# Moving work between engines and banks in a linear-attention and feed-forward kernel: last q on two engines, one load moved, single banks for two products

## The chip, the core and the metric

The kernel runs on one core of a Trainium2 chip. A core has TensorE (matrix products), VectorE, ScalarE and GpSimd (element by element), SyncE (issues transfers), 16 DMA engines, and a PSUM of 8 banks of 512 float32 columns into which TensorE writes. The metric is the device time of one execution in microseconds; the profile is of one such execution. In the profile's lines PE is TensorE, PEld its weight loads, DVE VectorE, ACT ScalarE, POOL GpSimd, SP SyncE; L594 is line 594 of the kernel before.

## What is computed

Linear attention with cosine weights, then a gated feed-forward block. Cut to what matters:

```python
# q, k, v: (8 batches, 8 heads, 576 positions, 64), float32
theta = pi / 2 * arange(576) / 576
phi(x) = concat([relu(x) * cos(theta), relu(x) * sin(theta)])       # 64 -> 128 features
kv  = einsum('bhsf,bhsd->bhfd', phi(k), v);  z = phi(k).sum(positions)
att = (phi(q) @ kv) / (phi(q) @ z + 1e-6)
x   = att.transpose(0, 2, 1, 3).reshape(4608, 512)
g   = x @ w_gate                                                     # 512 -> 1536
out = (g * sigmoid(g) * (x @ w_val)) @ w_out                         # -> (4608, 512)
```

## The kernel before

The 4608 tokens are 36 tiles of 128, four tiles to a **group**, groups 0 to 8. While TensorE does the feed-forward block of one group, the attention of later tiles is worked in between. The kernel hands out its work by **slots**: a group has 16, 12 for the gate and value products and 4 for the output products, and `at(slot, ...)` puts a piece of work behind the products of that slot, in program order on every engine. Batch b has `s0 = 16 * (b - 1)` and `p0 = s0 - 16`; a row of a table says in which slots its parts stand:

```python
# batch: (slots of q's weighting, slot of q's turning, slots of k's and v's preparation, all from p0; k-v product, from s0)
ROW = {2: ([16, 16, 17, 17], 18, (20, 21, 21, 22), 8), 3: ([12, 13, 14, 15], 18, (20, 20, 21, 21), 6), ...
       7: ([4, 4, 5, 5, 6, 6, ..., 12, 12], 15, (12, 13, 14, 15), 3)}
TILES = {2: (1, 9, 10, 11), 3: (5, 9, 10, 11), ...}      # slots of a group's four attention tiles
GATE = (5, 6, 7, 8)                                       # groups whose gate products go by quarters
AHEAD = 5
```

q is rectified and weighted with cos and sin into `r_q` (one buffer for all batches), and turned by a DMA transpose into `phit`. For batches 2 to 6 ScalarE rectifies and VectorE weights (`phi_q`, 4 of each); for batch 7 ScalarE does both in 18 parts:

```python
def phi_q_part(b, c, w):                                                                 # L296
    nc.scalar.activation(out=st[b, "q"][:, :, c, w], in_=raws[b, "q"][:, :, c], func=AF.Relu,
                         scale=csk[:, c, w:w + 1])                                       # L299
def qturn_dma(b, e):
    nc.sync.dma_start_transpose(out=phit[b][:, e]..., in_=st[b, "q"][e * 64:(e + 1) * 64]...)   # L322
```

The k-v product of a batch takes two neighbouring banks, half `e` in each; ScalarE and VectorE then copy it out, each from both banks:

```python
def kv_mm(b):
    ps = st[b, "kvps"] = take(2, ("kv", b))
    for j, c in ...:
        for i in range(2):
            for e in range(2):
                nc.tensor.matmul(out=ps[i * 64:(i + 1) * 64, e, ...], lhsT=raws[b, "k"]..., rhs=v2s...)  # L349
def kv_out2(b):
    def part(w, eng):
        for i in range(2):
            eng(out=kv2s[b % 2][w * 64:(w + 1) * 64, :, :, i], in_=ps[i * 64:(i + 1) * 64, :, :, w])     # L373
    part(0, nc.scalar.copy)
    if b - 1 in GATE:
        behind.append(lambda: (part(1, nc.vector.tensor_copy), kv_free(b)))
    else:
        part(1, nc.vector.tensor_copy)
```

An attention tile is 8 or 16 small products into two banks (`a_tile2`, L472), whose result VectorE divides into `x` (`x_of`: L486, L495, L499); a DMA transpose turns it into `xT` (`x_turn`, L578), which the feed-forward products of the next group read.

The feed-forward block of groups 1 to 4 (L594 products, L600 silu, L605 product with the value) and by quarters from group 5 on, with fewer products and more sums (`while behind` works off what was put into a list):

```python
def ffn_by_quarters(tg, slot_of):
    for u in range(3):
        product(a, ...); nc.scalar.copy(out=b, in_=a)             # products L652, copy L681
        product(e, ...); nc.scalar.copy(out=m7, in_=e)            # L685
        V(...); done()                                            # value products L665; done() works off a slot
        product(b, ...); nc.vector.tensor_tensor(out=c, in0=m7, in1=b, op=ALU.add)        # L691
        while behind: behind.pop(0)()
        product(a, ...); silu(u, 1, 0, a); V(...); done()         # silu: ScalarE, L658
        product(b, ...); nc.vector.tensor_tensor(out=m7, ...)     # L700
        while behind: behind.pop(0)()
        ...
        mul(u, 0, 0); mul(u, 1, 0)                                # VectorE, ht <- sg * value, L670
        ...
```

The output products (L767, from group 2 on by quarters, L826) end with the results in `ob` and eight stores to memory, from GpSimd's queue (L749). That queue also issues the loads of q, k and v of later batches:

```python
def load_behind(b):                       # in slot p0 + 3 (b < 5) or p0 + 1
    nc.gpsimd.tensor_copy(out=hold2, in_=phit[b - 1]...)          # L1038: waits for the turned q of the batch before
    if b < AHEAD: load(b, "q")
    if b > 3: load_kv(b)
    if AHEAD <= b + 1 < B: load(b + 1, "q")
```

Of the kernel before, what the change touches and what calls it, by code (L numbers as in the profile page):

```python
# [14 lines left out]
ALU = mybir.AluOpType  # L15
# [3 lines left out]
def kernel(  # L19
# [10 lines left out]
    nc = tc.nc  # L30
# [20 lines left out]
    KH = KC // 2  # L51
    GATE = (5, 6, 7, 8)
    AHEAD = 5
    WSUM = (32, 39, 49, 64)
    ROW = {2: ([16, 16, 17, 17], 18, (20, 21, 21, 22), 8), 3: ([12, 13, 14, 15], 18, (20, 20, 21, 21), 6), 4: ([12, 12, 12, 14], 15, (15, 16, 17, 18), 5), 5: ([12, 12, 12, 14], 15, (15, 16, 17, 17), 5), 6: ([6, 8, 11, 12], 14, (13, 14, 14, 17), 3), 7: ([4, 4, 5, 5, 6, 6, 7, 7, 8, 8, 9, 9, 10, 10, 11, 11, 12, 12], 15, (12, 13, 14, 15), 3)}
    TILES = {2: (1, 9, 10, 11), 3: (5, 9, 10, 11), 4: (5, 7, 9, 11), 5: (3, 4, 7, 9), 6: (0, 2, 5, 7), 7: (0, 1, 5, 7), 8: (0, 3, 5, 7)}
    FASTX = {}
    LATE = dict(M=44, V=87, O=131, X=26, x=150, v=(190, 250, 120, 150), e=130, a=90, c=170, b=110, k=120)

    consts = ctx.enter_context(tc.tile_pool(name="consts", bufs=1))  # L60
# [232 lines left out]
        nc.vector.tensor_tensor(out=st[b, "q"][:, g], in0=o.unsqueeze(2).to_broadcast([P, NC, 2, D]),  # L293
                                in1=tab, op=ALU.mult)

    def phi_q_part(b, c, w):  # L296
        if (b, "q") not in st:
            st[b, "q"] = rel.tile([P, G, NC, 2, D], BF16, name="r_q")
        nc.scalar.activation(out=st[b, "q"][:, :, c, w], in_=raws[b, "q"][:, :, c], func=AF.Relu,  # L299
                             scale=csk[:, c, w:w + 1])  # L300

# [38 lines left out]
                ps[:, 0:hi - lo].rearrange("p c (e s) -> p c e s", e=2))  # L340

    def kv_mm(b):
        ps = st[b, "kvps"] = take(2, ("kv", b))
        for j, c in [(j, c) for j in range(J) for c in range(NC)]:
            for i in range(2):
                for e in range(2):
                    es = slice(e * SH, (e + 1) * SH)
                    g = 2 * j + i
                    nc.tensor.matmul(  # L349
                        out=ps[i * D:(i + 1) * D, e, j * 2 * D1:(j + 1) * 2 * D1],  # L350
                        lhsT=raws[b, "k"][es, g, c],
                        rhs=v2s[b == 1][es, g, c, :, 0:D1],
                        start=(c == 0), stop=(c == NC - 1),
                    )
# [12 lines left out]

    def kv_out2(b):

        ps = st[b, "kvps"][:, :, 0:4 * J * D1 // 2].rearrange("p e (j w x) -> p e j w x", j=J, w=2)  # L370
        def part(w, eng):
            for i in range(2):
                eng(out=kv2s[b % 2][w * D:(w + 1) * D, :, :, i], in_=ps[i * D:(i + 1) * D, :, :, w])  # L373
# [195 lines left out]
        give_back(("xt", t, ks.start))  # L569

    def x_turn(t, fast=False):
        if t in FASTX:
            at(FASTX[t], lambda: (x_turn_pe(t), x_turned(t, "act")))
        elif fast:
            x_turn_pe(t)
            x_turned(t, "act")
        else:
            nc.sync.dma_start_transpose(out=xT_of(t), in_=st["x", t])  # L578
# [58 lines left out]
    def ffn_by_quarters(tg, slot_of):  # L637

        B11, B12, B21, B22 = x_parts(tg)
        val, gates, count = {}, {}, [0]  # L640

        def bank(nm, **kw):
            return take(1, ("g", tg, nm), **kw).rearrange("p (i x) -> p i x", i=2)

        def free(nm, late):
            give_back(("g", tg, nm), late)

        def product(to, u, a, x, first):
            rows[0] += LATE["M"]
            for i in range(2):  # L650
                for c in range(KH):
                    nc.tensor.matmul(out=to[:, i], lhsT=a[:, c, 2 * u + i], rhs=x[:, :, c],  # L652
                                     start=first and i == 0 and c == 0, stop=c == KH - 1, skip_group_check=True)

        def silu(u, w, j, src):
            if (u, w) not in gates:
                gates[u, w] = sg2p.tile([P, 2, T], BF16, name="sg2")
            nc.scalar.activation(out=gates[u, w][:, :, j * HT:(j + 1) * HT], in_=src, func=AF.Silu, scale=DOWN)  # L658

        def V(u, i, w):  # L660
            fc = 4 * u + 2 * i + w
            val[u, i, w] = take(1, ("v", tg, fc), fills=True)
            rows[0] += LATE["V"]
            for kc in range(KC):
                nc.tensor.matmul(out=val[u, i, w], lhsT=wv_sb[:, kc, fc * P:(fc + 1) * P], rhs=xT[tg][:, :, kc],  # L665
                                 start=(kc == 0), stop=(kc == KC - 1))

        def mul(u, i, w):
            fc = 4 * u + 2 * i + w
            nc.vector.tensor_tensor(out=ht[:, fc], in0=gates[u, w][:, i], in1=val.pop((u, i, w)), op=ALU.mult)  # L670
            give_back(("v", tg, fc), LATE["v"][2 * w + i])

        def done():
            slot_of(count[0])
            count[0] += 1

        for u in range(3):
            a = bank("a", fills=True)
            product(a, u, A11, B11, True)
            b = bank("b", seeded=True)  # L680
            nc.scalar.copy(out=b, in_=a)  # L681
            e = bank("e", fills=True)
            product(e, u, W3, X3, True)
            m7 = m7p.tile([P, 2, HT], FP32, name="m7")
            nc.scalar.copy(out=m7, in_=e)  # L685
            free("e", LATE["e"])
            V(*((u - 1, 1, 1) if u else (u, 0, 0)))
            done()
            product(b, u, W2, X2, False)
            c = bank("c", seeded=True)  # L690
            nc.vector.tensor_tensor(out=c, in0=m7, in1=b, op=ALU.add)  # L691
            while behind:
                behind.pop(0)()
# [12 lines left out]
            product(c, u, A22, X4, False)  # L706
            silu(u, 0, 0, c)
            free("c", LATE["c"])
            V(u, 1, 0) if u else V(u, 0, 1)
            done()  # L710
            if u == 2:
                token_sum(1, 0, 4)
            mul(u, 0, 0)
            mul(u, 1, 0)
            if u == 2:
                token_sum(3, 4, 6)
            product(b, u, W4, B22, False)
# [12 lines left out]
        mul(2, 1, 1)  # L730
        for n in (1, 2):
            token_sum(n, 4, 6)
        done()
# [182 lines left out]
    def at(s, *fns):  # L916
        plan.setdefault(s, []).extend(fns)
# [118 lines left out]
    def load_behind(b):  # L1036

        nc.gpsimd.tensor_copy(out=hold2, in_=phit[b - 1][0:1, :, 0, 0, 0])  # L1038
        if b < AHEAD:
            load(b, "q")  # L1040
        if b > 3:
            load_kv(b)
        if AHEAD <= b + 1 < B:
            load(b + 1, "q")

    def load_kv(b):
# [6 lines left out]
        load_kv(3)  # L1053


    for n in range(4):
        at(WSUM[n], lambda n=n: gate_weight_sum(n))
    for tg in GATE:
# [2 lines left out]
    for b in range(2, B):  # L1061
# [3 lines left out]
        phi, turned, weighed, kv_slot = ROW[b]  # L1065
        if b > 2:
            at(p0 + (3 if b < 5 else 1), lambda b=b: load_behind(b))
        if len(phi) > G:
            for i, s in enumerate(phi):
                at(p0 + s, lambda b=b, i=i: phi_q_part(b, *divmod(i, 2)))  # L1070
        else:
            for g, s in enumerate(phi):
                at(p0 + s, lambda b=b, g=g: phi_q(b, g))
# [2 lines left out]
        for e in range(2):  # L1076
            at(p0 + turned, lambda b=b, e=e: qturn_dma(b, e))
        at(s0 + kv_slot, lambda b=b: kv_mm(b), lambda b=b: kv_out2(b))
        if b - 1 not in GATE:
            at(s0 + kv_slot + 1, lambda b=b: kv_free(b))  # L1080
    at(SLOTS + 4, a_(8, 0))
    at(SLOTS + 5, a_(8, 1), turn(8))
    for tg in range(2, NTG):
        for i in range(tg == 2, OUT):
            t, s = tg * OUT + i, TILES[tg][i]
            later = tg - 1 in GATE and s in (0, 1, 3, 4, 7, 8)
            at(SLOTS * (tg - 1) + s, lambda t=t, later=later: (a_tile2(t, later), None if later else x_turn(t)))
            if t == 10:
                at(SLOTS * (tg - 1) + s, load_3)
# [50 lines left out]
```

## Time and profile before

| | |
|---|---|
| time, median of 3 runs | 313.88 us (313.21 to 314.5) |
| span of the profiled execution | 313.4 us |
| TensorE busy, products | 304.2 us (97%), 2768 |
| VectorE, ScalarE, GpSimd busy | 235.1, 153.4, 65.8 us |
| weighting of batch 7's q on ScalarE (L299), 128x256 | 18, 500 ns each |
| copies of the k-v products (L373), 64x260 | 12 on ScalarE, 374 ns; 12 on VectorE, 428 ns |
| loads of q, from issue to landing | median 11.8 us |
| turning of q (12) and of x (30), to landing | median 8.2 and 3.9 us |

How to read it: busy times of engines lie beside each other and don't add up to the span. Where one engine is busy nearly all the time, the others' idle time costs nothing as long as what they make is there when that engine asks for it. So the waits of the busiest engine count, and each is followed to what ended it: an operation, a bank that came free, or a transfer. A small operation of TensorE is listed longer than it holds the engine, since products overlap: times from start to start say what it takes.

### The profile page before, as it was taken

What the parts mean: (1) busy time and instruction counts of PE and PEld (TensorE: products, weight loads), DVE (VectorE), ACT (ScalarE), POOL (GpSimd) and SP (SyncE); (2) the same over time, 40 slices, a digit from 0 to 9 for tenths busy, and PEclk for the clock granted to TensorE, in tenths of its full rate; (3) what the DMA queues carried; (4) which work ended last, traced back from release to release, by engine and by line L of the source; (5) the groups of instructions that cost most, each with busy time, mean ns of one, the idle gap of its engine ahead of it and who ended that gap; (6) DMA issues with size and microseconds to landing.
All of it is one profiled execution on the core that took longest, in us unless ns stands there. A gap on an engine that the chain in (4) does not pass through costs nothing.

```text
span 313.4 us, 6940 instructions
## 1 busy us (share of the span) xinstructions
PE 304.2 (97%) x2768; PEld 196.7 (63%) x2768; DVE 235.1 (75%) x470; ACT 153.4 (49%) x290; POOL 65.8 (21%) x118
## 2 busy tenths in 40 slices
PE   8899999999999999999999999999999999999993
PEld 4587465445445485547654686568666876786683
DVE  7874777697777987687887887788879569955781
ACT  7454645663336355435545455796553254324530
POOL 7854102001520405030403031201400140032000
PEclk9999999999999999999999999999999999999999
DMA  7999998997799799989397979895920051013004
GB/s 270 217 198 197 207 204 132 227 136 100 126 230 117 123 200 142 193 106 188 70 195 84 201 119 158 115 153 78 222 39 17 2 151 36 17 37 100 2 0 135
DMA packets 72976, 41.08 MB, mean 131 GB/s; under 512 B 49904, under 2 KB 69872, under 8 KB 72944
## 3 DMA queue, kind: packets, MB, share of 16 engines
q0 software_dynamic: 24880, 24.91, 45.8%
q1 hardware_dynamic: 47472, 15.21, 31.3%
q10 hardware_dynamic: 592, 0.52, 0.5%
q8 instruction: 21, 0.34, 0.4%
q14 instruction: 11, 0.09, 0.1%
HBM read 37.75 MB, written 9.44 MB: 151 GB/s over the span
## 4 chain that ended last, share of the span: by engine, by line
PE 87%; DVE 6%; ACT 3%; DMA 2%; issue 1%; DVEq 0%; ACTq 0%
PE banks L594 32%; PE banks L826 18%; PE banks L665 13%; PE banks L652 11%; PE banks L767 6%; PE banks L349 3%; PE banks L472 2%; DMA xT<-x 2%; PE banks L522 1%; DVE x L499 1%; PE banks L453 1%; DVE v L303 1%; DVE ht L605 1%; DVE sums L798 1%; DVE raw_k L278 1%
## 5 line engine op out<-in xcount | busy, mean ns | idle before, releaser
L600 ACT ACTIVATE sg<-banks 128x512 bf16<-128x512 f32 (+2 forms) x68 | 37.1, 547 | 52.9 <-PE banks L594 49.9
L594 PE MATMUL banks<-xT,wg_sb 128*128 128x512 f16 (+2 forms) x272 | 62.1, 354 | 0.4 <-DMA xT<-x 0.4
L594 PE MATMUL banks<-xT,wv_sb 128*128 128x512 f16 (+2 forms) x272 | 62.0, 354 | 0.0
L605 DVE TENSOR_TENSOR ht<-sg,banks 128x512 f16<-128x512 bf16 (+2 forms) x68 | 41.7, 622 | 20.4 <-PE banks L594 13.2
L749 POOL DMA_DIRECT2D out_dram<-ob x56 | 29.3, 532 | 118.1 <-ACT ob L839 113.4
L665 PE MATMUL banks<-xT,wv_sb 128*128 128x512 f16 x192 | 48.6, 379 | 0.0
L594 PEld LDWEIGHTS <-wv_sb 128*128 128x128 f16 x272 | 26.0, 98 | 26.1
L594 PEld LDWEIGHTS <-wg_sb 128*128 128x128 f16 x272 | 24.7, 97 | 22.1 <-issue 0.7
L826 PEld LDWEIGHTS <-ht 128*128 128x128 f16 x336 | 32.7, 98 | 5.0
L670 DVE TENSOR_TENSOR ht<-sg,banks 128x512 f16<-128x512 bf16 x48 | 31.1, 682 | 4.0 <-ACT sg L658 4.0
L665 PEld LDWEIGHTS <-wv_sb 128*128 128x128 f16 x192 | 18.8, 98 | 13.3
L826 PEld LDWEIGHTS <-sums 128*128 128x128 f16 x252 | 24.6, 98 | 3.0
L658 ACT ACTIVATE sg<-banks 128x512 bf16<-128x512 f32 x36 | 20.3, 588 | 11.8 <-PE banks L652 11.8
L652 PEld LDWEIGHTS <-wgs_sb 128*128 128x128 f16 x192 | 17.8, 98 | 8.4 <-issue 1.5
L652 PE MATMUL banks<-kvt,wgs_sb 128*128 128x256 f16 x144 | 21.6, 273 | 1.3 <-ACT banks L681 0.9
L767 PE MATMUL banks<-wo_sb,ht 128*128 128x512 f16 x96 | 22.7, 380 | 0.0
L499 DVE TENSOR_TENSOR x<-banks,rec 128x512 f16<-128x512 f32 (+1 forms) x32 | 21.6, 674 | 1.3 <-PE banks L453 0.3
L826 PE MATMUL banks<-wo_sb,ht 128*128 128x256 f16 x168 | 20.6, 273 | 0.0
L303 DVE TENSOR_TENSOR v<-raw_v,tab 128x1152 bf16<-128x1152 bf16 x27 | 19.7, 754 | 0.5 <-ACT raw_v L889 0.5
L826 PE MATMUL banks<-wt_sb,sums 128*128 128x256 f16 x168 | 19.5, 273 | 0.0
L826 PE MATMUL banks<-wt_sb,ht 128*128 128x256 f16 x168 | 19.5, 273 | 0.0
L839 ACT ACTIVATE ob<-banks 128x512 f32<-128x512 f32 x14 | 8.4, 597 | 21.9 <-PE banks L826 21.9
(123 smaller groups left out, 407.9 us busy)
## 6 DMA issues: line engine op xcount, KB each, us to landing
out_dram<-ob POOLq DMA_DIRECT2D x56, 128.0 KB, 4.9
raw_k<-in_k_dram POOLq DMA_DIRECT2D x7, 576.0 KB, 6.7
raw_q<-in_q_dram POOLq DMA_DIRECT2D x6, 576.0 KB, 11.8
raw_v<-in_v_dram POOLq DMA_DIRECT2D x6, 576.0 KB, 10.0
wo_sb<-in_moe_w_out_dram POOLq DMA_DIRECT2D x3, 512.0 KB, 12.8
out_dram<-ob SPq DMA_DIRECT2D x11, 128.0 KB, 6.0
wg_sb<-in_moe_w_gate_dram POOLq DMA_DIRECT2D x5, 256.0 KB, 8.9
wv_sb<-in_moe_w_val_dram POOLq DMA_DIRECT2D x5, 256.0 KB, 9.8
```

Source lines behind the costliest of these rows:

```text
L303: nc.vector.tensor_tensor(out=v2s[b == 1][:, g, :, :, 0:D], in0=(first if b == 0 and g == 0 else {"v": raw_of(b, "v")})["v"][:, g].unsquee ...
L499: nc.vector.tensor_tensor(out=st["x", t].rearrange("p (y e d) -> p e y d", e=2, d=D)[:, :, ys], in0=ps[:, :, 0:2 * J * D1].rearrange("p e ...
L594: nc.tensor.matmul(out=st["f", tg, fc, lo][i], lhsT=(wg_sb, wv_sb)[i][:, kc, fs], rhs=xT[tg][:, ts, kc], start=(kc == 0), stop=(kc == KC - 1))
L600: nc.scalar.activation(out=sg[:, 0:n], in_=st["f", tg, fc, lo][0], func=AF.Silu, scale=DOWN)
L605: nc.vector.tensor_tensor(out=ht[:, fc, r:r + n], in0=st.pop(("s", tg, fc, lo))[:, 0:n], in1=ps[1], op=ALU.mult)
L652: nc.tensor.matmul(out=to[:, i], lhsT=a[:, c, 2 * u + i], rhs=x[:, :, c], start=first and i == 0 and c == 0, stop=c == KH - 1, skip_group_ ...
L658: nc.scalar.activation(out=gates[u, w][:, :, j * HT:(j + 1) * HT], in_=src, func=AF.Silu, scale=DOWN)
L665: nc.tensor.matmul(out=val[u, i, w], lhsT=wv_sb[:, kc, fc * P:(fc + 1) * P], rhs=xT[tg][:, :, kc], start=(kc == 0), stop=(kc == KC - 1))
L670: nc.vector.tensor_tensor(out=ht[:, fc], in0=gates[u, w][:, i], in1=val.pop((u, i, w)), op=ALU.mult)
L749: (queues or (nc.sync, nc.sync))[e].dma_start(out=out_v[idx // NC, idx % NC][:, cols], in_=ob_of(t)[e * SH:(e + 1) * SH, cols])
L767: nc.tensor.matmul(out=o_ps[t], lhsT=ht[:, fc, r:r + P], rhs=wo_sb[:, fc], start=(fc == 0), stop=(fc == FC - 1))
L826: nc.tensor.matmul(out=to[i][:, 0] if len(to) == 2 else to[0][:, i], lhsT=a[:, kc, i * P:(i + 1) * P], rhs=b[:, kc], start=first and kc == ...
```

## The change

It has three named parts, and with them slots in the tables move.

- The q of the last batch is weighted half by ScalarE (cosine parts, 9, from slot 6) and half by GpSimd (sine parts, 9, all in slot 4), to take work from ScalarE in group 5.
- The first q that is loaded a batch ahead, that of batch 5, is issued at the end of group 2, behind the group's stores, no longer together with the q, k and v of batch 4. This takes a transfer out of the time in which group 2's tiles are turned.
- The k-v products of batches 2 and 5 take two single banks, not a pair. ScalarE copies out one bank and VectorE the other, in four copies each, and each bank is given back as soon as it is copied.

Beside that, pieces of work move by one to three slots: the gate weight sums, tile 13 (group 3's second, from slot 9 to 8 of group 2), q's weighting of batches 3, 4, 6 and 7, its turning, and k's and v's preparation. A third place works off the list `behind`; `LATER` holds in a table, for every group, the slots that were written out before.

```diff
-    WSUM = (32, 39, 49, 64)
-    ROW = {2: (...), 3: ([12, 13, 14, 15], 18, (20, 20, 21, 21), 6), 4: ([12, 12, 12, 14], 15, (15, 16, 17, 18), 5), 5: ([12, 12, 12, 14], 15, (15, 16, 17, 17), 5), 6: ([6, 8, 11, 12], 14, (13, 14, 14, 17), 3), 7: ([4, 4, 5, 5, ..., 12, 12], 15, (12, 13, 14, 15), 3)}
-    TILES = {2: (1, 9, 10, 11), 3: (5, 9, 10, 11), ...}
-    FASTX = {}
+    WSUM = (29, 38, 48, 64)
+    ROW = {2: (...), 3: ([12, 12, 13, 13], 18, (17, 20, 21, 21), 6), 4: ([12, 12, 14, 14], 14, (13, 16, 17, 18), 5), 5: ([12, 12, 12, 14], 14, (14, 16, 17, 17), 5), 6: ([6, 8, 11, 12], 12, (13, 14, 15, 18), 3), 7: ([6, 6, 7, 7, ..., 14, 14], 16, (12, 13, 14, 15), 3)}
+    TILES = {2: (2, 9, 10, 11), 3: (5, 8, 10, 11), ...}
+    FIRST_AHEAD = 15
+    MIXED = {7: 4}
+    KVONE = (2, 5)
+    LATER = {2: (0, 1, 3, 4, 7, 8), ..., 8: (0, 1, 3, 4, 7, 8)}
...
-    def phi_q_part(b, c, w):
+    def phi_q_part(b, c, w, pool=False):
...
+        if pool:
+            nc.gpsimd.tensor_scalar(out=st[b, "q"][:, :, c, w], in0=raws[b, "q"][:, :, c], scalar1=0.0,
+                                    scalar2=csk[:, c, w:w + 1], op0=ALU.max, op1=ALU.mult)
+            return
...
     def kv_mm(b):
-        ps = st[b, "kvps"] = take(2, ("kv", b))
+        if b in KVONE:
+            ps = st[b, "kvps"] = [take(1, ("kv", b, e)) for e in range(2)]
+        else:
+            both = st[b, "kvps"] = take(2, ("kv", b))
+            ps = [both[:, e] for e in range(2)]
...
     def kv_out2(b):
+        if b in KVONE:
+            for e, eng in enumerate((nc.scalar.copy, nc.vector.tensor_copy)):
+                ps = st[b, "kvps"][e][:, 0:4 * J * D1 // 2].rearrange("p (j w x) -> p j w x", j=J, w=2)
+                for w in range(2):
+                    for i in range(2):
+                        eng(out=kv2s[b % 2][w * D:(w + 1) * D, e, :, i], in_=ps[i * D:(i + 1) * D, :, w])
+                give_back(("kv", b, e))
+            return
...
             mul(u, 0, 0)
             mul(u, 1, 0)
+            while behind:
+                behind.pop(0)()
...
-        if AHEAD <= b + 1 < B:
+        if AHEAD < b + 1 < B:
             load(b + 1, "q")
...
+    at(SLOTS * (AHEAD - 3) + FIRST_AHEAD, lambda: load(AHEAD, "q"))
...
-        if len(phi) > G:
+        if b in MIXED:
+            for c in range(NC):
+                at(p0 + phi[2 * c], lambda b=b, c=c: phi_q_part(b, c, 0))
+                at(p0 + MIXED[b], lambda b=b, c=c: phi_q_part(b, c, 1, True))
+        elif len(phi) > G:
```

More of the change, by code (lines that the diff above doesn't have):

```diff
@@ L53 @@
     AHEAD = 5
-    WSUM = (32, 39, 49, 64)
-    ROW = {2: ([16, 16, 17, 17], 18, (20, 21, 21, 22), 8), 3: ([12, 13, 14, 15], 18, (20, 20, 21, 21), 6), 4: ([12, 12, 12, 14], 15, (15, 16, 17, 18), 5), 5: ([12, 12, 12, 14], 15, (15, 16, 17, 17), 5), 6: ([6, 8, 11, 12], 14, (13, 14, 14, 17), 3), 7: ([4, 4, 5, 5, 6, 6, 7, 7, 8, 8, 9, 9, 10, 10, 11, 11, 12, 12], 15, (12, 13, 14, 15), 3)}
-    TILES = {2: (1, 9, 10, 11), 3: (5, 9, 10, 11), 4: (5, 7, 9, 11), 5: (3, 4, 7, 9), 6: (0, 2, 5, 7), 7: (0, 1, 5, 7), 8: (0, 3, 5, 7)}
-    FASTX = {}
+    WSUM = (29, 38, 48, 64)
+    ROW = {2: ([16, 16, 17, 17], 18, (20, 21, 21, 22), 8), 3: ([12, 12, 13, 13], 18, (17, 20, 21, 21), 6), 4: ([12, 12, 14, 14], 14, (13, 16, 17, 18), 5), 5: ([12, 12, 12, 14], 14, (14, 16, 17, 17), 5), 6: ([6, 8, 11, 12], 12, (13, 14, 15, 18), 3), 7: ([6, 6, 7, 7, 8, 8, 9, 9, 10, 10, 11, 11, 12, 12, 13, 13, 14, 14], 16, (12, 13, 14, 15), 3)}
+    TILES = {2: (2, 9, 10, 11), 3: (5, 8, 10, 11), 4: (5, 7, 9, 11), 5: (3, 4, 7, 9), 6: (0, 2, 5, 7), 7: (0, 1, 5, 7), 8: (0, 3, 5, 7)}
+    FIRST_AHEAD = 15
+    MIXED = {7: 4}
+    KVONE = (2, 5)
+    LATER = {2: (0, 1, 3, 4, 7, 8), 3: (0, 1, 3, 4, 7, 8), 4: (0, 1, 3, 4, 7, 8), 5: (0, 1, 3, 4, 7, 8), 6: (0, 1, 3, 4, 7, 8), 7: (0, 1, 3, 4, 7, 8), 8: (0, 1, 3, 4, 7, 8)}
     LATE = dict(M=44, V=87, O=131, X=26, x=150, v=(190, 250, 120, 150), e=130, a=90, c=170, b=110, k=120)
@@ L349, in kv_mm @@
                     nc.tensor.matmul(
-                        out=ps[i * D:(i + 1) * D, e, j * 2 * D1:(j + 1) * 2 * D1],
+                        out=ps[e][i * D:(i + 1) * D, j * 2 * D1:(j + 1) * 2 * D1],
                         lhsT=raws[b, "k"][es, g, c],
@@ L571, in x_turn @@
     def x_turn(t, fast=False):
-        if t in FASTX:
-            at(FASTX[t], lambda: (x_turn_pe(t), x_turned(t, "act")))
-        elif fast:
+        if fast:
             x_turn_pe(t)
@@ L1078 @@
         at(s0 + kv_slot, lambda b=b: kv_mm(b), lambda b=b: kv_out2(b))
-        if b - 1 not in GATE:
+        if b - 1 not in GATE and b not in KVONE:
             at(s0 + kv_slot + 1, lambda b=b: kv_free(b))
@@ L1085 @@
             t, s = tg * OUT + i, TILES[tg][i]
-            later = tg - 1 in GATE and s in (0, 1, 3, 4, 7, 8)
+            later = tg - 1 in GATE and s in LATER[tg - 1]
             at(SLOTS * (tg - 1) + s, lambda t=t, later=later: (a_tile2(t, later), None if later else x_turn(t)))
```

## The prediction

> **What bounds the kernel now.** I read the page first, then the waits of TensorE, then the stretches where those waits lie, with the timeline of the engine that ends each.
>
> From the page, busy time and the 40 slices:
>
> ```profile
> PE 304.2 (97%) x2768; PEld 196.7 (63%) x2768; DVE 235.1 (75%) x470; ACT 153.4 (49%) x290; POOL 65.8 (21%) x118
> ...
> PE   8899999999999999999999999999999999999993
> ...
> DMA  7999998997799799989397979895920051013004
> ```
>
> TensorE is busy in every slice but the first two and the last; the other engines have room. The change leaves TensorE's 2768 products as they are and moves one group of 8 past its neighbours, so it can only take away idle time of TensorE. The waits of TensorE say how much there is once the start is over:
>
> ```profile
> PE banks L652 <- ACT banks L681: 0.9, 1, 0.9
> PE banks L652 <- DVE x L499: 0.4, 1, 0.4
> PE banks L594 <- DMA xT<-x: 0.4, 1, 0.4
> PE banks L349 <- DVE ht L670: 0.3, 1, 0.3
> ```
>
> These are counted from the modelled end of a product. Counted from start to start, against what such products take back to back (216 ns at 512 columns, 109 ns at 256, about 32 ns at 65), each comes out about 0.16 us longer, and that is what the end can gain: 1.02, 0.57, 0.57 and 0.49 us. One more of 0.23 us stands before the products at 202.6. Together 2.88 us, in two places. Two equal stretches, group 5 and group 6 of eight tiles each, show the larger one (columns: stretch, length, then busy time of PE, PEld, DVE, ACT, POOL, clock, DMA share, GB/s):
>
> ```profile
> 185.50:218.90 33.40, 31.74 (x324) 23.44 (x322) 26.52 (x51) 22.90 (x49) 6.09 (x12) 1.00 0.92 128
> 218.90:250.10 31.20, 31.20 (x330) 23.07 (x329) 24.37 (x47) 13.41 (x25) 4.15 (x9) 1.00 0.38 71
> ```
>
> The same products take 2.2 us more in group 5, and what differs is ScalarE, 22.90 against 13.41 us. Its timeline there, and TensorE's:
>
> ```profile
> 199.39 0.91 ACT L299 ACTIVATE r_q<-raw_q,cs_all 128x256 bf16<-128x256 bf16 x2 [2.09 <-DMA xT<-x]
> ...
> 202.47 0.90 ACT L299 ACTIVATE r_q<-raw_q,cs_all 128x256 bf16<-128x256 bf16 x2
> 203.27 0.58 ACT L681 COPY banks<-banks 128x512 f32<-128x512 f32 x1
> ```
>
> ```profile
> 202.62 0.42 PE L472 MATMUL banks<-kv,phit 128*128 128x65 bf16 x8
> 203.90 0.60 PE L652 MATMUL banks<-kvt,wgs_sb 128*128 128x256 f16 x4 [0.86 <-ACT banks L681]
> ```
>
> ScalarE comes to the first q weighting (L299) 2.09 us before it may write r_q, which a transfer still reads; the silu behind it are late by that much, two more weightings stand ahead of the copy L681, and TensorE waits for the copy. The other place is the start of group 3, where TensorE needs the last turned tile:
>
> ```profile
> 118.94 1.47 PE L826 MATMUL banks<-wo_sb,sums 128*128 128x256 f16 x12
> 120.82 0.38 PE L594 MATMUL banks<-xT,wg_sb 128*128 128x512 f16 x1 [0.40 <-DMA xT<-x]
> ```
>
> In the chain that ended last, and in the table of stretches, the reason stands:
>
> ```profile
> 114.34 6.34 DMA xT<-x
> ```
>
> ```profile
> 106.00:110.00 4.00, 4.00 (x41) 1.99 (x40) 3.83 (x9) 1.19 (x2) 0.34 (x1) 1.00 1.20 204
> 110.00:114.00 4.00, 4.00 (x41) 3.21 (x40) 3.79 (x11) 1.30 (x3) 0.00 (x0) 1.00 1.21 207
> 114.00:118.00 4.00, 4.00 (x39) 3.58 (x37) 3.06 (x6) 2.78 (x5) 0.00 (x0) 1.00 1.24 194
> ```
>
> VectorE, nearly full (3.8 of 4 us), finishes that x at 114.3; the turning then takes 6.34 us against a median of 3.9 us for all 30, because four loads issued together at 103.3 to 106.3 fill the DMA until 118.
>
> **What the Trainium skill says.** "DMA: Bandwidth & Descriptors", Queues, rings and completion order: each DMA engine goes round the queues that have work, packet by packet. So a turning beside loads gets only its turns; the 6.34 against 3.9 us agrees. "SBUF — State Buffer", SBUF: two separate sides: GpSimd and a VectorE operation with two SBUF inputs take a shared port pair one after the other, whole instruction by whole instruction. No view of this kernel shows it: GpSimd has hardly any arithmetic. "GPSIMD Engine Reference", Elementwise — side-by-side cycle accounting: 1.8 to 2.6 cycles an element at 1.2 GHz. My estimate for a 256-column weighting from that is 0.38 to 0.55 us and some start-up. The nearest thing in the trace, a 128x128 select on GpSimd, took 0.29 us, which fits.
>
> **The change part by part.**
>
> 1. Last batch's q. ScalarE loses 9 of its 18 weightings at 0.45 us each in a pair (0.91 for two): 4.0 us less in group 5. The first one comes two places later, after the four silu of the second third, when r_q is free (199.4; it would be reached at about 202). So the wait of 2.09 us goes, and one weighting instead of two stands ahead of L681. Saved at TensorE: 1.02 + 0.23 = 1.25 us. The 9 on GpSimd start after its two loads, near 201.5 (199.4 and about 2 us of issuing); at 0.5 to 1 us each they end by 206 to 211. They are off the path unless they last beyond 217.
>
> 2. First q ahead. The load of q5 leaves the four at 103 and goes behind the eight stores of group 2, to about 124. Three loads remain; at some 3.5 us each the DMA comes free near 115 instead of 118. Beside that the weight sum L627 (0.87 us net) moves ahead of VectorE's last gap (0.21 us idle at 103.4), where one vmul of 0.66 us had been moved away too, and x of that tile should be done about 0.8 us earlier, at 113.5. Even with 6.34 us it would land at 119.9; with an ordinary 3.9 us at 117.4. TensorE is ready at 120.25. Saved: 0.57 us, the whole wait.
>
> 3. k-v products of batches 2 and 5 in single banks. VectorE's two copies waited 1.2 us for ScalarE's two (three times in the waits, 3.6 us). Now each engine has its own bank and both start at once, but with four copies of 130 columns instead of two of 260. The two forms before (374 ns at 260, 580 ns at 512 on ScalarE) give about 0.8 ns a column, so some 0.27 us for 130 and 1.1 us for four instead of 0.76. The product is whole some 0.3 us earlier on VectorE's side. On TensorE's path that is 0.09 us at 73.1 for batch 2 and nothing for batch 5.
>
> 4. The two other waits in group 5 stay, 0.57 and 0.49 us. Both are waits for a bank: the first for the x of a tile in the same bank, which VectorE starts only when TensorE has made it (191.4), the second for the third of three ht behind it. From the code the banks of group 5 are handed out as before and VectorE keeps that order.
>
> The other table entries move work inside idle time; the second place to empty the list of late work finds the list empty, and LATER holds what was written out before. Sum: 1.25 + 0.57 + 0.09 = 1.9 us, from 313.88 to 312.0.
>
> **Rivals.**
>
> - The turning of the last q becomes the wait. Before, ScalarE ended its part and the turning went out at 213.8, ahead of the stores (218.5). Now the last weighting stands behind the copy at 217.6, so the turning goes out near 218.5 minus what was saved, among the stores. The same meeting for batch 6 took from 182.3 to 199.4, 17 us; here TensorE needs it at 234.7 minus the same saving, 16 us later. For it: those numbers. Against it: other batches took 10.5 to 14 us. It would give back up to 1 us: 313.
> - q5 now runs beside the turning of q4 and puts off what waits for that, the loads of k5, v5, q6, from 134 to perhaps 137. They would end near 150 and could hold the last x of group 3, needed at 153.2. Some 2 us of margin; it could give back 0.5 us.
> - GpSimd is slow, or locks VectorE out. Were a weighting 2 us, they would end near 219.5 and hold the turning 1 or 2 us; at 5 us, a loss of over 10 us. Only a short VectorE operation with two SBUF inputs (0.68 us at 203.2) meets them early, so I don't expect the lock to matter.
> - The two bank waits go too, if VectorE comes early enough. That would give another 1 us: 311.
>
> **Range and chances.** 1.9 us less, with 0.1 us held back for the first two rivals weighed by a quarter and a tenth: 312.1 us. The low end is one of the bank waits gone; the high end is one rival taking most of the gain, plus some 0.4 us for the spread of few runs (313.2 to 314.5 before). Two per cent is 6.3 us, more than twice all idle time found, so faster by that much is nearly excluded; slower needs GpSimd several times slower than estimated.
>
> **What would show it.** TensorE's waits without L681 and without the turned tile at group 3; the last xT of group 2 landing before 119; 9 GpSimd operations of 0.5 to 1 us between 201 and 212; the first ScalarE weighting of batch 7 without a wait; group 5 near 32.1 us; the two bank waits still there. It is wrong if a new wait stands at the turning of batch 7 (near 233), at the start of group 4, or after a lock between GpSimd and VectorE, or if TensorE's waits go and the time doesn't.

## The result and the profile after

The changed kernel is **slower by 0.6%**: 316.06 us median of 6 runs (315.38 to 317.05) against 314.25 us for the kernel before on the same chip (313.21 to 314.78), ratio 1.0064 [1.0041, 1.0087]. Predicted were 312.1 us, and 311.2 to 313.4 us as the range. Run again on another chip it gave 1.0032 [1.0021, 1.0043], so the sign is sure and the size lies between 0.3 and 0.6%. The profiled spans are 314.7 us after and 313.4 us before; they belong to executions of 316.45 and 315.17 us, so the account below is of 1.3 us between two executions, where the medians lie 1.8 us apart.

The lines moved: L594 is now L611, L652 is L669, L665 is L682, L472 is L491, L670 is L687, L681 is L698, L499 is L518, L826 is L845, L798 is L817, L322 is L329, L1038 is L1057, L141 is L144, L839 is L858, L349 is L360, L373 is L392; L303 is GpSimd's weighting and L386 are the single-bank copies of both engines. First the page after, busy time and slices:

```profile
PE 304.0 (97%) x2768; PEld 196.9 (63%) x2768; DVE 236.6 (75%) x474; ACT 150.8 (48%) x285; POOL 76.1 (24%) x127
...
PE   8899999999999999999899999999999999999992
```

TensorE does the same work in the same busy time. One slice in the middle, the twentieth (149 to 157 us), has lost its 9. The waits of TensorE after (in total, times, longest):

```profile
PE banks L611 <- DMA xT<-x: 1.0, 1, 1.0
PE banks L491 <- DMA phit<-r_q: 0.8, 1, 0.8
...
PE banks L669 <- DVE x L518: 0.4, 1, 0.4
PE banks L360 <- DVE ht L687: 0.3, 1, 0.3
PE banks L845 <- DVE sums L817: 0.3, 1, 0.3
```

The wait for the copy (L681 before) is gone, and the two bank waits (L669, L360) stand as before. Three are new. L611 looks like the old wait for a turned tile, but lies elsewhere. The timeline of TensorE shows the places:

```profile
140.19 0.30 PE L491 MATMUL banks<-kv,phit 128*128 128x65 bf16 x4 [0.79 <-DMA phit<-r_q]
...
154.34 1.04 PE L611 MATMUL banks<-xT,wg_sb 128*128 128x512 f16 x4 [0.96 <-DMA xT<-x]
...
213.57 0.61 PE L845 MATMUL banks<-wt_sb,sums 128*128 128x256 f16 x4 [0.32 <-DVE sums L817]
```

Counted from start to start, as in the prediction, the three are 0.95, 1.12 and 0.48 us, 2.55 us together. Gone are 1.25 us at 202, 0.57 us at 120 and 0.09 us at 73: 1.91 us. The balance is +0.64 us. The last twelve products start at 307.62 us against 307.13 us, 0.49 us later, so −0.15 us of small differences remain:

```profile
307.13 1.47 PE L826 MATMUL banks<-wo_sb,sums 128*128 128x256 f16 x12
307.62 1.47 PE L845 MATMUL banks<-wo_sb,sums 128*128 128x256 f16 x12
```

The first line is of the kernel before. From there to the end of the span it took 7.08 us after (314.7 − 307.62) and 6.27 us before: **another 0.81 us is lost after TensorE's last wait.** 0.49 and 0.81 us make the 1.3 us between the spans.

Group 5 and group 6 in the table of stretches:

```profile
186.80:219.50 32.70, 31.64 (x325) 23.38 (x323) 27.71 (x52) 19.30 (x39) 16.38 (x21) 1.00 0.84 113
219.50:250.70 31.20, 31.20 (x330) 23.13 (x328) 24.32 (x48) 13.70 (x26) 4.21 (x9) 1.00 0.52 90
```

Group 5 is 0.70 us shorter than before (33.40), though 1.25 us of waiting went: the 0.48 us at 213 lie in it. The loss around 140 and 154 is seen on GpSimd's queue, which issues loads and stores:

```profile
124.51 0.80 POOL L144 DMA_DIRECT2D raw_q<-in_q_dram  x1
140.29 0.42 POOL L1057 COPY hold<-phit 1x2 bf16<-1x2 bf16 x1 [14.99 <-DMA phit<-r_q]
```

The first line is the load that was moved. The second is the small copy that waits for the turned q of batch 4. In the kernel before it ran at 133.82:

```profile
133.82 0.17 POOL L1038 COPY hold<-phit 1x2 bf16<-1x2 bf16 x1 [9.62 <-DMA phit<-r_q]
```

Behind it stand the loads of k5, v5 and q6, issued at 140.8 to 143.1 instead of 134.4 to 136.7. The chain that ended last runs through the same transfers:

```profile
127.03 13.11 DMA phit<-r_q
...
146.72 7.58 DMA xT<-x
```

First the turning of q4, beside the load, then the turning of the last tile that group 4 begins with, beside the three loads that had to wait for q4.

### The profile page after: what moved, and what is told of

Same layout as the page of the kernel before. It is cut to its first block, busy times and chain, and to the rows that moved or that the text cites. A ratio compares the mean times of both kernels' runs of the same rounds, so it can differ in the third digit from the quotient of the medians.

```text
span 314.7 us, 6944 instructions
## 1 busy us (share of the span) xinstructions
PE 304.0 (97%) x2768; PEld 196.9 (63%) x2768; DVE 236.6 (75%) x474; ACT 150.8 (48%) x285; POOL 76.1 (24%) x127
## 4 chain that ended last, share of the span: by engine, by line
PE 81%; DVE 7%; DMA 7%; ACT 2%; SPq 2%; issue 1%; DVEq 0%; ACTq 0%
PE banks L611 28%; PE banks L845 16%; PE banks L682 12%; PE banks L669 11%; PE banks L786 6%; DMA phit<-r_q 4%; DMA xT<-x 2%; PE banks L360 2%; PE banks L491 2%; SPq L329 2%; DVE ht L687 2%; DVE x L518 1%; PE banks L541 1%; PE banks L472 1%; DVE v L310 1%
## 5 line engine op out<-in xcount | busy, mean ns | idle before, releaser
L611 PE MATMUL banks<-xT,wg_sb 128*128 128x512 f16 (+2 forms) x272 | 62.0, 354 | 1.0 <-DMA xT<-x 1.0
L611 PE MATMUL banks<-xT,wv_sb 128*128 128x512 f16 (+2 forms) x272 | 62.0, 354 | 0.0
L682 PE MATMUL banks<-xT,wv_sb 128*128 128x512 f16 x192 | 48.6, 379 | 0.0
L611 PEld LDWEIGHTS <-wv_sb 128*128 128x128 f16 x272 | 26.1, 98 | 26.1
L611 PEld LDWEIGHTS <-wg_sb 128*128 128x128 f16 x272 | 24.7, 98 | 22.7 <-DMA xT<-x 1.2
L845 PEld LDWEIGHTS <-ht 128*128 128x128 f16 x336 | 32.7, 98 | 4.8
L687 DVE TENSOR_TENSOR ht<-sg,banks 128x512 f16<-128x512 bf16 x48 | 31.0, 679 | 3.3 <-ACT sg L675 3.3
L682 PEld LDWEIGHTS <-wv_sb 128*128 128x128 f16 x192 | 18.8, 98 | 13.3
L845 PEld LDWEIGHTS <-sums 128*128 128x128 f16 x252 | 24.6, 98 | 3.5 <-DVE sums L817 0.6
L518 DVE TENSOR_TENSOR x<-banks,rec 128x512 f16<-128x512 f32 (+1 forms) x32 | 21.6, 674 | 1.3 <-PE banks L472 0.3
L669 PEld LDWEIGHTS <-wgs_sb 128*128 128x128 f16 x192 | 17.8, 98 | 7.4 <-issue 0.6
L669 PE MATMUL banks<-kvt,wgs_sb 128*128 128x256 f16 x144 | 21.6, 273 | 0.4 <-DVE x L518 0.4
L845 PE MATMUL banks<-wo_sb,ht 128*128 128x256 f16 x168 | 20.6, 273 | 0.0
L845 PE MATMUL banks<-wt_sb,sums 128*128 128x256 f16 x168 | 19.7, 273 | 0.3 <-DVE sums L817 0.3
L845 PE MATMUL banks<-wt_sb,ht 128*128 128x256 f16 x168 | 19.5, 273 | 0.0
L858 ACT ACTIVATE ob<-banks 128x512 f32<-128x512 f32 x14 | 8.4, 597 | 22.4 <-PE banks L845 22.4
## 6 DMA issues: line engine op xcount, KB each, us to landing
raw_q<-in_q_dram POOLq DMA_DIRECT2D x6, 576.0 KB, 11.2
```

Of the source, the lines that this page charges most:

```text
L518: nc.vector.tensor_tensor(out=st["x", t].rearrange("p (y e d) -> p e y d", e=2, d=D)[:, :, ys], in0=ps[:, :, 0:2 * J * D1].rearrange("p e ...
L611: nc.tensor.matmul(out=st["f", tg, fc, lo][i], lhsT=(wg_sb, wv_sb)[i][:, kc, fs], rhs=xT[tg][:, ts, kc], start=(kc == 0), stop=(kc == KC - 1))
L845: nc.tensor.matmul(out=to[i][:, 0] if len(to) == 2 else to[0][:, i], lhsT=a[:, kc, i * P:(i + 1) * P], rhs=b[:, kc], start=first and kc == ...
```

## The experiments

All ratios are to the kernel before, run on the same chip, with a 95% interval. "End" is the time from the start of the last twelve products to the end of the span.

**The load alone, both ways.** First the changed kernel with only its load of q5 put back:

```diff
-        if AHEAD < b + 1 < B:
+        if AHEAD <= b + 1 < B:
-    at(SLOTS * (AHEAD - 3) + FIRST_AHEAD, lambda: load(AHEAD, "q"))
```

> The changed kernel with one thing undone: the load of batch 5's q goes back to the other three at the start of group 2. Theory A (the moved load runs among the stores and the turning of batch 4's q, so that turning, and behind it three loads and the last x of group 3, come late): TensorE's waits at 139.2 (0.95 us) and 153.1 (1.12 us) go, 2.07 us, and none comes back at the start of group 3, since the loads of group 2 now begin 3 us earlier: about 314.0 us, 2 us under the changed kernel, level with or a little under the kernel before. Theory B (the loss comes from GpSimd locking VectorE out): the same time as the changed kernel, within 0.3 us.

Measured: 0.9977 [0.9963, 0.9991], 314.05 us. Both waits are gone, and the small copy is early:

```profile
134.78 0.18 POOL L1057 COPY hold<-phit 1x2 bf16<-1x2 bf16 x1 [10.19 <-DMA phit<-r_q]
```

There is no wait at the start of group 3 either, though the load is back among the four: what else the change does, the table moves above all, had been enough to get that tile turned in time. It isn't always: of the five later versions with the load put back, one (a tile in slot 1) has 0.50 us there. The wait varies in the kernel before too: 0.57 us in its profile, 0.36 and 0.40 us in the two with copies added in the last group. Then the kernel before with only the load moved:

```diff
-        if AHEAD <= b + 1 < B:
+        if AHEAD < b + 1 < B:
+    at(SLOTS * 2 + 15, lambda: load(AHEAD, "q"))
```

> The kernel before with the moved load alone. Theory A: the wait of 0.57 us at the start of group 3 goes, two new ones of about 0.95 and 1.1 us come, at the turned q of batch 4 and at the start of group 4: 1.5 us slower than before, ratio 1.005. Theory B: 0.6 us faster, ratio 0.998.

Measured: 1.0055 [1.0034, 1.0076], 316.18 us. The 0.57 us at group 3 went, so the load move is enough for that as well; but the copy ran at 139.63 us (133.82 before), and the start of group 4 lost more, 2.15 us, than the start of group 3 had gained. The 0.95 us expected at the turned q did not come: that product waited 0.1 us.

```profile
139.63 0.18 POOL L1038 COPY hold<-phit 1x2 bf16<-1x2 bf16 x1 [14.66 <-DMA phit<-r_q]
```

```profile
154.71 1.04 PE L594 MATMUL banks<-xT,wg_sb 128*128 128x512 f16 x4 [1.99 <-DMA xT<-x]
155.58 1.45 PE L594 MATMUL banks<-xT,wv_sb 128*128 128x512 f16 x4
156.83 1.91 PE L594 MATMUL banks<-xT,wg_sb 128*128 128x512 f16 x4
```

Four products of 512 columns take 1.04 us in the first line and 1.91 us in the third, at half speed, for some 3.4 us: about 1.6 us more on top of the wait. This is the slowest of the nine executions (317.73 us; seven of them took 316.0 to 316.42), so the slowed stretch is likely not in most of them. The two runs together show that the load move by itself makes the wait at 153, and that without it there is none at 139. How long the one at 139 is turns on a few tenths: TensorE comes there at 139.1 to 139.3, and the small copy that waits for the same turned q ran at 139.6 here and at 140.3 in the changed kernel.

**A third place for the load**, ahead of the turning of q4: held back by a copy that reads the turned tile of group 2, ahead of the stores.

```diff
-    at(SLOTS * (AHEAD - 3) + FIRST_AHEAD, lambda: load(AHEAD, "q"))
+    def load_ahead():
+        nc.gpsimd.tensor_copy(out=hold2, in_=xT[3][0:1, 3, 0, 0:2])
+        load(AHEAD, "q")
+    at(SLOTS * 2 + 12, load_ahead)
```

> The changed kernel with the load of batch 5's q neither at the start of group 2 nor behind its stores, but held until the last x of group 2 is turned (near 116 us), ahead of the stores, where the transfers stood idle for some 4 us. Theory A: it is done near 120.5, q of batch 4 is turned by about 135 as without the move, and the waits at 139 and 153 go: as fast as the changed kernel with the load put back, ratio to before 0.996 to 0.998. Rival: if any load between the groups delays the stores and with them the turning, the waits stay and it is no faster than 1.002.

Measured: 0.9974 [0.9964, 0.9984]. The load was issued at 117.62 us and landed at 123.6 (the first of the two transposes that turn q4 went out at 121.9), and the copy that waits for q4 ran at 135.58 us, 0.8 us later than with the load put back; TensorE waited at neither place. So it isn't the load ahead that costs, but that it was issued at 124.5, 2.8 us after the first and 2.5 us ahead of the second transpose of q4. It gains nothing over putting it back.

**GpSimd's half.** The changed kernel with all 18 weightings on ScalarE:

```diff
-    MIXED = {7: 4}
+    MIXED = {}
```

> The changed kernel with all 18 weightings of the last q on ScalarE, in the same late slots, and none on GpSimd. Theory A: VectorE's sums of two SBUF operands between 207 and 212 go back from 0.75 to 0.98 us to 0.42 and 0.69 us, and TensorE's wait of 0.48 us at 213 goes; up to 0.4 us comes back at the copy at the start of the last third, behind two weightings instead of one: 0 to 0.5 us faster than the changed kernel. Theory B: it gains most of the loss, 1.5 us or more.

Measured: 1.0028 [1.0002, 1.0055]. The wait at 213 went, and the timeline of VectorE shows why. In the changed kernel, beside GpSimd (the first line is GpSimd's):

```profile
203.00 10.23 POOL L303 TENSOR_SCALAR r_q<-raw_q,cs_all 128x256 bf16<-128x256 bf16 x9
...
203.71 0.68 DVE L817 TENSOR_TENSOR sums<-ht 128x1024 f16<-128x1024 f16 x1
...
207.66 0.98 DVE L817 TENSOR_TENSOR ht<-ht 128x1024 f16<-128x1024 f16 x1
...
209.87 0.75 DVE L817 TENSOR_TENSOR sums<-ht 128x512 f16<-128x512 f16 x1
```

In this run, with GpSimd idle:

```profile
207.40 0.69 DVE L817 TENSOR_TENSOR ht<-ht 128x1024 f16<-128x1024 f16 x1
...
209.32 0.42 DVE L817 TENSOR_TENSOR sums<-ht 128x512 f16<-128x512 f16 x1
```

The first three of the five sums from 207.7 on, which have two inputs in SBUF, are stretched by 0.2 to 0.3 us each while GpSimd weights; the products between them, which read a bank, are not, and neither is the sum at 203.71. There was no wait at the copy L698 either, so in the changed kernel the later slots alone would do for that wait; what GpSimd's half is worth can't be read from this run, since its end was long (6.90 us; see below).

The kernel before with part 1 only (the halves, with `phi_q_part` as in the change, and the slots of q7):

```diff
-    ROW = {..., 7: ([4, 4, 5, 5, ..., 12, 12], 15, (12, 13, 14, 15), 3)}
+    ROW = {..., 7: ([6, 6, 7, 7, ..., 14, 14], 16, (12, 13, 14, 15), 3)}
+        if b == 7:
+            for c in range(NC):
+                at(p0 + phi[2 * c], lambda b=b, c=c: phi_q_part(b, c, 0))
+                at(p0 + 4, lambda b=b, c=c: phi_q_part(b, c, 1, True))
```

> The kernel before with the last q's weighting alone changed: 9 parts on ScalarE from slot 6, 9 on GpSimd. Theory A: the 1.25 us at the copy at 203 goes, 0.5 us comes at the sums: 0.75 us faster, ratio 0.9976. If the lock were the main loss: no faster or slower than before.

Measured: 0.9974 [0.9962, 0.9987], 313.95 us. The 1.25 us went, a wait of 0.41 us for VectorE's sums came. Part 1 by itself is a gain. The profile is 1.5 us shorter than that of the kernel before, more than these two waits give; the wait at group 3 (0.29 us) and the end (6.08 us) happen to be shorter too.

**Four of nine on GpSimd**, with the load put back, so that GpSimd is done before the sums begin:

```diff
-                at(p0 + MIXED[b], lambda b=b, c=c: phi_q_part(b, c, 1, True))
+                if c < 4:
+                    at(p0 + MIXED[b], lambda b=b, c=c: phi_q_part(b, c, 1, True))
+                else:
+                    at(p0 + phi[2 * c], lambda b=b, c=c: phi_q_part(b, c, 1))
```

> The changed kernel with the load of batch 5's q put back, and only four of the nine weightings on GpSimd (the other five stay on ScalarE, in the late slots). Theory A, with the lock as a smaller term: GpSimd is done near 205.6 at 1.13 us each, before VectorE's sums of two SBUF operands at 205.7 to 210, which take 0.69 and 0.42 us again, and TensorE's wait of 0.5 us at 211 goes: 0.5 us under the version with all nine, ratio to before 0.996. Rival, that five more weightings on ScalarE hold its copies: no gain or a loss of up to 0.5 us.

Measured: **0.9948 [0.9929, 0.9967]**, 313.31 us, the best of all. From GpSimd's timeline:

```profile
200.80 4.99 POOL L303 TENSOR_SCALAR r_q<-raw_q,cs_all 128x256 bf16<-128x256 bf16 x4
```

GpSimd is done at 205.8, where the first of the sums starts (205.82 us), and that takes 0.69 us. Of TensorE's waits after the start only the two bank waits are left, 0.58 and 0.49 us.

**The single banks.** The changed kernel with pairs for all k-v products again:

```diff
-    KVONE = (2, 5)
+    KVONE = ()
```

> The changed kernel with the k-v products of batches 2 and 5 in a pair of banks again. Theory A and B: no difference beyond 0.2 us, the 0.09 us wait at 73 may come back. A rival, that the other order of banks or the eight more copies cost time somewhere the waits don't show: 0.5 us or more faster.

Measured: 1.0012 [1.0001, 1.0023]. GpSimd's nine weightings took 11.2 us here, not 10.2, and TensorE didn't wait for the sums: GpSimd seems to be the one that waited. Its two weightings beside the sums at 203.16 and 207.11 took 1.57 and 1.64 us, and those sums their usual 0.68 and 0.69. Beside it stands the changed kernel itself, run again without an edit:

> The changed kernel once more, beside the next three on one chip. Theory A: slower than the kernel before by what was seen (1.0041 to 1.0087), with the waits near 139 and 153 us of 0.4 to 1.5 us each, which move from execution to execution as the transfers fall.

Measured: 1.0032 [1.0021, 1.0043], with 0.27, 1.35 and 0.46 us at the three new waits.

The best version (four of nine, load put back) with the same edit, `KVONE = ()`:

> The version with the load put back and four weightings on GpSimd, with pairs of banks again for batches 2 and 5. If single banks do nothing: ratio to before as that version, 0.995 within 0.001. Rival: single banks cost, 0.993.

Measured: 0.997 [0.9958, 0.9981], beside 0.9948 with single banks; the intervals overlap. And the kernel before with single banks alone, `kv_mm` and `kv_out2` as in the change:

```diff
+    KVONE = (2, 5)
```

> The kernel before with single banks for the k-v products of batches 2 and 5 alone. As in the prediction: the 0.09 us at 73 us goes, VectorE no longer waits 1.2 us for ScalarE there, and the time is the same within 0.1%, ratio 0.999 to 1.001. Rival, since the changed kernel with pairs came out 0.2% under the changed kernel: single banks cost, ratio 1.002.

Measured: 1.0029 [1.0012, 1.0046], where a gain of 0.09 us was the whole of what I had reckoned. So the one part leans to a gain in the best version and to a loss in the other two. Little of this is in TensorE's waits that belong to the single banks (0.09 us at 73 goes or comes). Others differ too, and whether by the banks is open: the changed kernel with pairs has none at 139 and none for the sums, where its repeat has 0.27 and 0.46. In the last run 0.76 us instead of 0.23 us stand at 202; that is no sign of the banks, for the two kernels below that are the kernel before up to 280 us have 0.35 and 0.85 there. What differs most is the end, single banks against pairs: 6.55 and 7.08 us against 6.12 in the changed kernel, 6.98 against 6.27 in the kernel before, but 6.11 against 6.66 in the best version.

**The end of the kernel.** Over all 18 profiles the end goes with the number of ScalarE's instructions on the page:

| ScalarE instructions | end, us | kernels |
|---|---|---|
| 281 | 6.08, 6.12 | before with part 1; changed with pairs |
| 285, 286 | 6.55 to 7.08 | changed (twice), load put back, load at 117; best with pairs |
| 289, 290 | 6.08 to 6.27 | before, best, and six others |
| 294 | 6.90 to 7.15 | changed with q on ScalarE, before with single banks, and one below |

To test it, four copies of one column were added on ScalarE in the last group, in slots where it is idle:

```diff
+    for s in (0, 3, 6, 9):
+        at(SLOTS * 8 + s, lambda: nc.scalar.copy(out=tiny, in_=half_pi))
```

The expectations count all that ScalarE is given, with what only issues or waits (452 where the page has 285), and take the end from the start of the last single product, which is 1.2 us later. In the changed kernel (285 to 289):

> The changed kernel with four added one-column ScalarE copies in the last group, where ScalarE has room. Theory, that the fetch of ScalarE's instructions among the last stores lengthens the end: 452 instructions become 456, the fetch comes earlier, and from the last product's start to the end it takes 4.9 to 5.0 us, not 5.3 to 5.9: 0.4 to 0.9 us faster than the changed kernel, ratio to before 1.001 to 1.002. Rival, that the length of the end is chance or comes from what the change does: no faster, 1.003 or more.

In the kernel before (290 to 294):

> The kernel before with the same four ScalarE copies: 457 become 461, the fetch falls 2.6 us before the last product's start, and the end takes about 5.75 us: 0.7 us slower, ratio 1.002 to 1.0025. Rival: 1.000.

As a control, in the kernel before on VectorE, so that ScalarE's number stays:

```diff
+    for s in (0, 3, 6, 9):
+        at(SLOTS * 8 + s, lambda: nc.vector.tensor_copy(out=tiny, in_=half_pi))
```

> Control: the kernel before with four one-column copies on VectorE in the same places. ScalarE's stream is as it was, the end stays at 5.0 us: ratio 1.000 within 0.001.

And in the changed kernel with the load put back (285 to 289), nine weightings still on GpSimd:

> The changed kernel with the load put back, all nine weightings on GpSimd, and the four ScalarE copies. It tells how much of the gain of the version with four weightings on GpSimd (0.9948) came from its longer ScalarE stream and not from the lock. Theory: the end at 4.9 us takes 0.5 us off 0.9977, so 0.996, and the lock's 0.5 us is still there. Rival: 0.9977 as before.

Measured: the changed kernel 1.0012 [0.9997, 1.0027], end 6.08 us; the kernel before 1.0028 [1.0017, 1.004], end 7.15 us; the control 1.0009 [0.9992, 1.0027], end 6.12 us; the load put back 0.9951 [0.993, 0.9971], end 6.22 us. Four operations more **shorten** the end of the changed kernel by 0.5 or 1.0 us (against its two profiles) and of the third by 0.4 us, and lengthen that of the kernel before by 0.9 us. In the lengthened one ScalarE's timeline has this:

```profile
305.26 3.07 ACTq L756 DMA_DIRECT2D out_dram<-ob  x2
308.37 0.60 ACT L839 ACTIVATE ob<-banks 128x512 f32<-128x512 f32 x1 [3.14 <-issue]
```

The issue of two stores takes 3.07 us where it took 2.00 us in the kernel before, and the activation behind it comes 1 us later (308.37, not 307.39) with no product or buffer to wait for. What fits in time is a queue that brings instructions, one of two in the trace, in packets of 8 KB. The last of these packets starts 2.6 us before the last product does (294 instructions), or 0.8 to 0.9 us after it (289, 290), 2.5 to 2.7 us after it (285, 286), or 5.4 to 5.7 us (281). So with 294 it would stand in ScalarE's way; with 285 and 286 it falls beside the last stores, which end late. That the number of ScalarE's instructions moves the end is shown by the added copies; that the fetch is the means is read from these times and not tested.

The last of these runs also bears on the lock, the taking of turns between GpSimd and VectorE. Load put back with nine weightings on GpSimd and a short end gave 0.9951; with four weightings and a short end 0.9948. The wait of 0.5 us for the sums is there in the first and not in the second, and the profiled spans are 311.8 and 311.4 us, but the intervals don't tell the times apart. Against the profile of the load put back (312.3 us) the four weightings have 0.55 us less at the end and 0.50 us less waiting, so about half of what four for nine seemed to bring over 0.9977 was the end.

**The bank waits.** The first of the two that stay, at group 5's third slot, was tried by moving the second attention tile that is worked in group 5 (slot 2 in the table) one slot up and one down, in the best version:

```diff
-    TILES = {..., 6: (0, 2, 5, 7), ...}
+    TILES = {..., 6: (0, 1, 5, 7), ...}      # and (0, 3, 5, 7)
```

> The version with the load put back and four weightings on GpSimd, and the second attention tile of group 6 worked in slot 1 of group 5, not 2. It takes on the two waits that no part of the change touched (0.58 us for the bank of that tile's result at 191.4, 0.49 us at the k-v product behind it): VectorE gets the tile 1.7 us earlier and the bank is free before TensorE asks. Both waits go: 1.0 us less, ratio 0.9915. Rival: VectorE is full there and the wait only moves, 0.995.

> The same version with that tile in slot 3, behind the k-v product, where the next products take other banks. Both waits go too if the bank is the cause: ratio 0.9915 to 0.993; a new wait for VectorE behind the k-v product may take half of it back.

Measured: 0.9966 [0.9954, 0.9978] and 1.0018 [1.0008, 1.0028]. In the first the wait at 191 went, and 0.62 us came at 189 for the x of the tile before, and the wait at the k-v product grew from 0.49 to 0.97 us (0.50 us stand at group 3 as well, far from there):

```profile
PE banks L360 <- DVE ht L687: 0.8, 1, 0.8
```

In the second the k-v copies became the wait:

```profile
PE banks L682 <- DVE kv L392: 1.3, 1, 1.3
```

The program takes the free bank that was used longest ago, and here VectorE is the one that returns them. In both runs another bank was late in place of the first.

## Why the prediction was wrong

- **Part 1, ScalarE relieved: right.** 1.25 us went in the changed kernel and with part 1 alone, where 0.41 us of waiting for the sums stand against it (0.9974). The exact size was in part luck: 0.23 us of the 1.25 us are a wait that took up to 0.85 us in other profiles of the same code.
- **GpSimd's durations: too low.** The trace has 1.13 us for each 256-column weighting (median of 9; range 1.129 to 1.253), not 0.5 to 1 us, and they lasted from 203.0 to 213.2 us, not from 201.5 to between 206 and 211. My estimate from "GPSIMD Engine Reference", Elementwise — side-by-side cycle accounting, was 0.38 to 0.55 us; the operation here does a maximum and a product with a column, and costs at least twice that.
- **The lock: the step that dismissed it failed.** I had counted one short operation of VectorE with two SBUF inputs in the way. From 207.7 to 213.5 there are five sums, the first three stretched, and the last of them feeds TensorE: 0.48 us. "SBUF — State Buffer", SBUF: two separate sides, gives the shared ports to whichever starts first, for its whole instruction. The trace agrees that only operations with two SBUF inputs suffer, but those are stretched by 0.2 to 0.3 us only: the sum at 209.87 started with one of GpSimd's weightings (209.87 to 211.00) and, by the profile's times, was over at 210.62, ahead of it.
- **Part 2, the load: its gain right, its price mis-sized.** The 0.57 us went, but went without the load move too. The rival had been named: the load beside the turning of q4 puts off k5, v5 and q6 to 137, with "some 2 us of margin", half a microsecond at a tenth. **This is the step that failed, and the main error.** I added one load's share of the DMA, 3 us, to the end of the turning. It took 5.8 us (load alone) and 6.5 us (all of the change) longer, so the margin of 2 us was not only used up; TensorE itself needed the turned q at 139.2. Cost: 2.07 us in this profile. It varies: in the repeated run the two waits were 0.27 and 1.35 us.
- **Part 3: the 0.09 us were there, the rest not seen.** VectorE's four copies of 130 columns took 1.23 us (I had 1.1) and no longer wait 1.19 us for ScalarE. Its price, or gain, stands mostly at the end, which goes with the number of ScalarE's instructions.
- **The end: not in the prediction at all.** I took the time from the last product to the end for fixed. It moved by 0.81 us.
- **Rival of q7's turning: right that it stays hidden.** The product that reads it (235.3 us) had no wait. **The bank waits: right**, both stayed.

The sum by the prediction's own terms: −1.91 us predicted and found; +2.07 us for the load's price, +0.48 us for the lock, +0.81 us at the end, −0.15 us of small differences, together +1.3 us of span. Open are the means by which the end moves, and why the waits at 139, 153 and 202 differ from profile to profile.

## What to carry to other kernels

A load moved out of one crowded stretch goes into another: look up the transfer that runs at the new place, who waits for it, and who is queued behind that one, and reckon with its lengthening by more than the load's own time (here 5.8 us where 3 us were reckoned). Before giving GpSimd arithmetic, list every VectorE operation with two SBUF inputs in its stretch, and give it only as much as is done before the first; here that was worth about 0.5 us of waiting. When a change of a fraction of a per cent is judged, split the span at the start of the last products: here the number of instructions on another engine was worth as much as the waits that the change was about, and adding four idle copies to ScalarE shows it.

## What the runs showed of the hardware

- **The end and instruction fetch.** "Runtime: NRT & Kernel Launch", Instruction fetch mechanics, says that each engine's instructions are fetched in blocks while it runs, mostly hidden. Here the end of the kernel took 6.1 to 6.3 us or 6.5 to 7.15 us, by four instructions of ScalarE. If a fetch is the means, it isn't hidden there; no run tests that.
- **TensorE's clock after a short wait.** After a wait of 2.15 us (the kernel before with the load moved, one execution), the granted clock was about half in a stretch of 3.2 us, as the table of stretches has it:

```profile
156.00:159.20 3.20, 3.20 (x9) 1.17 (x8) 2.06 (x3) 1.37 (x3) 0.53 (x2) 0.51 1.20 158
```

The 0.51 is the clock, 1.00 in the other stretches shown. The wait at the same place brought nothing of the kind at 1.12 us in the changed kernel, nor at 1.50 us in the changed kernel with q on ScalarE.
- **A turning beside a load.** The turning of q4 ended 5.8 us later with one load of 576 KB issued 3 us after the first of its two transposes (the load moved alone, against the kernel before), and 0.8 us later with the same load issued 4.3 us ahead of that transpose (the third place, against the load put back).
